# Block-sorted attention and a residual MLP: exponentials from rows of scores, turned by transposing DMAs

## The chip, the cores and the metric

One Trainium2 chip, one of its cores. The metric is the device time of one execution in microseconds. The engines of a core are PE (matrix products), DVE (vector), ACT (activations), POOL (here element-wise sums and the issue of loads) and SP (which here only issues DMAs). Each engine works through its own instructions in order; they wait for each other and for DMAs by semaphores.

## What is computed

Four batches, eight heads, 768 tokens, 64 columns per head; the tokens form 8 blocks of 96. `P` is an 8x8 matrix per head, made from `sort_net` by five rounds of normalising rows and columns.

```python
k_sorted = np.einsum('bhij,bhjcd->bhicd', P, k_b)      # blocks of k and v mixed by P
v_sorted = np.einsum('bhij,bhjcd->bhicd', P, v_b)
scores = scale * np.matmul(q_b, k_sb.transpose(0, 1, 2, 4, 3))   # 96x96 in each block
scores = scores - np.max(scores, axis=-1, keepdims=True)
attn = np.exp(scores)
attn = attn / (np.sum(attn, axis=-1, keepdims=True) + 1e-09)
x = np.matmul(attn, v_sb)                              # then heads side by side: 768x512
# residual MLP
a1 = alpha1 * x + beta1
tok = np.einsum('ts,bsd->btd', w_tok, a1)              # 768x768 over the tokens
u = x + lam * tok
a2 = alpha2 * u + beta2
ch = np.maximum(a2 @ w_ch1, 0.0) @ w_ch2               # 512 -> 2048 -> 512
out = u + lam * ch
```

## The kernel before

The batches run in a pipeline written out by hand. Batch 0's attention opens the program. Then, for b = 0, 1, 2, the function `both` does two thirds of the MLP of batch b (`hidden` for its first half of tokens, three `result` tiles, `hidden` for its second half) and, woven into it, the attention of batch b+1. After that `join` does the last three `result` tiles of batch b together with the token mix (`token_mix`) of batch b+1, and woven into that, `ahead` mixes the blocks of k and v of batch b+2. The MLP of batch 3 ends the program alone.

`weave(main, other, ratio)` sets the order: each step of a generator yields a cost, and after each step of `main` steps of `other` are recorded until their costs reach `ratio` times those of `main`. The costs only place instructions in the engines' queues; they delay nothing by themselves.

Attention of a batch, before. Heads are handled in pairs `p` = 0 to 3 (heads p and p+4 on the two halves of the partitions), and blocks in groups `g` of four. `score` computes q times k for eight 96x96 blocks into a PSUM bank pair `psA` (two exist, `bankA` takes them in turn), with the queries on the partitions; DVE reduces their maxima into `mx` (L453). When all eight scores of the batch are done, `split_max` and `turn_max` write the maxima as two bfloat16 parts and turn them (L474 to L482). Then `soft` computes the scores a second time with the keys on the partitions (L508), subtracts each query's maximum by a second product, with a mask of -1 (L515), and ACT takes eight 96x96 exponentials in one instruction into `ET` (L520). `value` multiplies `ET` by the sorted v, whose extra column of ones gives the sums (L534), and DVE divides into `x16` (L546, L547). The token mix reads `x16` (L609).

`hidden` makes one of 16 tiles of 128 hidden columns in each step: four products into one of the three PSUM banks of `psM` (L674), and a relu that empties the bank, on ACT (L684), for every fourth tile on DVE (L682). In stage 0, the first half's `hidden` also turns the second half of u (`u_turn`, with its activation L645 on ACT). `result` sums 16 products of 512 columns (L712), and two DVE instructions and an output store on SP follow (L721 to L723).

SP's queue holds, in one order, the output stores, the transposing DMAs for `a2T` (L656, after ACT's cast of u, L651), those for `qT` (`q_send`, L343), and `v_relay`, which sends the sorted v through DRAM to its place in `vS` (L430, L436). The loads of k, v and q of batch b+2 are issued by POOL behind a small copy, `gate` (L850), in the middle of `both`.

Of the kernel before, what the change touches and what calls it, by code (L numbers as in the profile page):

```python
# [10 lines left out]
FT = mybir.dt.float32  # L11
F16 = mybir.dt.float16
BF = mybir.dt.bfloat16
AF = mybir.ActivationFunctionType
ALU = mybir.AluOpType
# [5 lines left out]
def kernel(  # L21
# [18 lines left out]
    B, H, S, D = q.shape  # L40
    NB = sort_net.shape[-1]
    BLK = S // NB
# [20 lines left out]
    def wt(shape, dtype, name):  # L63
        return wts.tile(shape, dtype, name=name, tag=name)
# [4 lines left out]
    def tmp(shape, dtype, name, bufs):  # L69
        return work.tile(shape, dtype, name=name, tag=name, bufs=bufs)  # L70

    turn_A, turn_M = count(), count()

    def bankA():
        return psA.tile([128, 2, 512], FT, name="psA", tag=f"psA{next(turn_A) % 2}")

    def bank(pool, dtype=FT):
        n = 512 if dtype is FT else 1024
        tag = "psM" if pool is psM else "psX"
        return pool.tile([128, n], dtype, name=tag, tag=tag)  # L80
# [11 lines left out]
    kT = wt([128, H4 * S + 32], F16, "kT")  # L92
    qT = [[wt([128, S + 32], F16, f"qT{n}_{p}") for p in range(H4)] for n in range(2)]
    vS = two([BLK, 64, VP], F16, "vS")
    ET = [wt([BLK, 2, NB, GAP], F16, f"ET{n}") for n in range(2)]
    x16 = two([128, NT, C], F16, "x16")
    mh = wt([BLK, 2, 2, H4 * NB], BF, "mh")
    E0 = [ET[0][:], ET[1][:]]
    for home in (
        x16[1][0:BLK].rearrange("p s c -> p (s c)"),  # L100
        raw0[0:BLK, 0:2 * NB * GAP],
    ):
        E0.append(home.rearrange("p (l i c) -> p l i c", l=2, c=GAP))
    u = {}
    u16 = wt([128, NT, C], BF, "u16")
    w_tokT = wt([128, NT, S], BF, "w_tokT")
# [1 line left out]
    W2 = wt([128, HT, C], BF, "W2")  # L108
    PB = [wt([128, 2, 2, H4, NB], F16, f"PB{b}") for b in range(B)]

    def load_k(b):
        G.dma_start(rawk[0:64, :], k[b].rearrange("h (j t) d -> (h j) (t d)", j=NB)[:, 0:HALF * D])
        G.dma_start(rawk[64:128, :], k[b].rearrange("h (j t) d -> (h j) (t d)", j=NB)[:, HALF * D:])

    def load_v(b, halves=(0, 1)):
        src = v[b].rearrange("h (j t) d -> (h j) (t d)", j=NB)
        if b == 0:
            G.dma_start(raw0[0:64], src)
            return
        for th in halves:  # L120
            G.dma_start(
                rawv[th * 64:(th + 1) * 64, :], src[:, th * HALF * D:(th + 1) * HALF * D]
            )
# [46 lines left out]

    load_v(1, (0,))
    for home in E0[1:3]:
        G.memset(home[:, :, :, BLK:], 0.0)
    for quarter in range(4, 16):
        if quarter == 12:
            load_v(1, (1,))
# [7 lines left out]
        for p in range(H4):  # L184
            V.memset(qT[n][p][:, S:], 0.0)
    V.memset(v0T[:, BLK * D:], 0.0)
    V.memset(ET[0][:, :, :, BLK:], 0.0)
    ones_bf = wt([128, 1], BF, "ones_bf")
    V.memset(ones_bf[:], 1.0)

# [7 lines left out]
    mx0 = wt([BLK, 2, 2, H4 * NB], FT, "mx0")  # L198
    V.memset(mx0[:], 0.0)
    mx1 = wt([BLK, 2, H4 * NB], FT, "mx1")  # L200
    mx = [mx0[:, :, 0], mx1[:]]
    tp = [wt([128, BLK], BF, f"tp{n}") for n in range(2)]
    tp_of = {}
# [142 lines left out]
            )  # L346

    def q_two(b, p, eng):
        ps = psA.tile([128, 2, 1024], F16, name="psA", tag=f"psA{next(turn_A) % 2}")
        q_turn(b, p, ps[:, 0])  # L350
        q_turn(b, p + 1, ps[:, 1])
        q_copy(b, p, ps[:, 0], A)
        q_copy(b, p + 1, ps[:, 1], eng)
# [88 lines left out]
    def score(b, p, g):  # L442
        ps = bankA()
        for i in range(4):
            for hl in range(2):
                r = slice(hl * 64, hl * 64 + 64)
                c = (g * 4 + i) * BLK
                PE.matmul(  # L448
                    ps[:, hl, i * BLK:(i + 1) * BLK], qT[b % 2][p][r, c:c + 128],
                    kT[r, p * S + c:p * S + c + BLK], start=True, stop=True,  # L450
                )
        c = p * NB + g * 4
        V.tensor_reduce(  # L453
            mx[b % 2][:, :, c:c + 4],
            ps[0:BLK, :, 0:4 * BLK].rearrange("p l (i t) -> p l i t", t=BLK), AXX, ALU.max,
        )

    def score_one(b, p, g, hl):
        ps, r = bank(psM), slice(hl * 64, hl * 64 + 64)
# [9 lines left out]
            ps[0:BLK, 0:4 * BLK].rearrange("p (i t) -> p i t", t=BLK), AXX, ALU.max,  # L469
        )  # L470

    def split_max(b):
        m = mx[b % 2]
        V.tensor_copy(mh[:, :, 0], m)  # L474
        V.tensor_tensor(mh[:, :, 1], m, mh[:, :, 0], ALU.subtract)

    def turn_max(b):
        ps = bank(psX, BF)
        PE.transpose(
            ps[:, 0:BLK], mh[:].rearrange("p l e c -> p (l e c)"), identbf[0:BLK, 0:BLK]  # L480
        )
        V.tensor_copy(tp[b % 2][:], ps[:, 0:BLK])  # L482
        for p in range(H4):
            tp_of[p] = tp[b % 2]

    def turn_first(p, n):
        ps = bank(psX)
        PE.transpose(
# [8 lines left out]
            )  # L497

    def exps(b, p):
        return ET[p % 2] if b > 0 else E0[p]  # L500

    def soft(b, p, g):
        ps = bankA()
        for i in range(4):
            c = (g * 4 + i) * BLK
            for hl in range(2):
                r = slice(hl * 64, hl * 64 + 64)
                PE.matmul(  # L508
                    ps[:, hl, i * BLK:(i + 1) * BLK], kT[r, p * S + c:p * S + c + 128],
                    qT[b % 2][p][r, c:c + BLK], start=True, stop=False, skip_group_check=True,  # L510
                )
            for hl in range(2):
                r = slice(hl * 64, hl * 64 + 64)
                n = p * NB + g * 4 + i
                PE.matmul(  # L515
                    ps[:, hl, i * BLK:(i + 1) * BLK],
                    nmask[r, n:n + 1].to_broadcast([64, 128]), tp_of[p][r, :],
                    start=False, stop=True, skip_group_check=True,
                )
        A.activation(  # L520
            exps(b, p)[:, :, g * 4:(g + 1) * 4, 0:BLK],
            ps[0:BLK, :, 0:4 * BLK].rearrange("p l (i t) -> p l i t", t=BLK),
            AF.Exp, scale=scale,
        )

    def products(b, p, hl, ps):
        h = hl * H4 + p
        E = exps(b, p)[:, hl].rearrange("p i c -> p (i c)")
        for s in range(NT):
            b0, s3 = s // 3 * 4 + s % 3, s % 3  # L530
            for half in range(2):
                i = b0 + half
                c0 = i * GAP + (32 * s3 if half == 0 else 32 * s3 - BLK)
                PE.matmul(  # L534
                    ps[:, s * VP:s * VP + D + 1], E[:, c0:c0 + 128],
                    vS[b % 2][:, h * NB + i, 0:D + 1],
                    start=(half == 0), stop=(half == 1), skip_group_check=True,
                )
# [14 lines left out]
    def attention(b):  # L553
        yield 0.7
        if b + 1 < B:
            big_p(b + 1)
            yield 0.1
        for p in range(H4):
            for g in range(2):
                score(b, p, g)  # L560
            yield 0.65
        split_max(b)
        yield 0.9
        turn_max(b)
        yield 0.5
        for p in range(H4):
            for g in range(2):
                soft(b, p, g)
            yield 0.9
            if p > 0:  # L570
                value(b, p - 1)
                yield 1.1
        yield 0.5
        value(b, H4 - 1)

    def ahead(b):
# [93 lines left out]
    def hidden(b, half):  # L670
        for m in range(HT):
            ps = bank(psM)
            for ci in range(CT):
                PE.matmul(  # L674
                    ps[:, 0:TOK], W1[:, ci, m * 128:(m + 1) * 128], a2T_of[b, half][:, ci, :],
                    start=(ci == 0), stop=(ci == CT - 1),
                )
            if m % 2 == 0:
                pair = tmp([128, S], BF, "hT", 10)
            t = hT_of[m] = pair[:, m % 2 * TOK:(m % 2 + 1) * TOK]  # L680
            if m % 4 == 3:
                V.tensor_scalar(t, ps[:, 0:TOK], 0.0, None, op0=ALU.max)  # L682
            else:
                A.activation(t, ps[:, 0:TOK], AF.Relu)  # L684
            if b == 0 and half == 0 and m in (5, 7, 9, 11):
                u_turn(b, 1, (m - 5) // 2)
            yield 0.65
# [80 lines left out]
    q_pair(0, 3, psM, A)  # L768
    v_first(3, A, psM)
    v_first_layout(0, 3, A)  # L770
    G.memset(E0[3][:, :, :, BLK:], 0.0)
    load_q(1)
    load_k(1)
    for ci in range(CT):
# [59 lines left out]
    for b in range(B):  # L834
# [8 lines left out]
            break  # L843

        def both(b=b):
            yield from hidden(b, 0)
            for kk in range(3):
                yield from result(b, 0, kk, b if b > 0 and kk == 1 else None, 1)
                if kk == 1 and b + 2 < B:
                    G.tensor_copy(  # L850
                        gate[:], a2T_of[b, 1][0:1, CT - 1, 0:1] if b else vS[1][64:65, 63, 0:1]
                    )
                    load_v(b + 2)
                    load_k(b + 2)
                    load_q(b + 2)
            yield from hidden(b, 1)
            if b + 2 < B:
                q_send(b + 2)

        weave(both(), attention(n), 0.42)  # L860

        def join(b=b, n=n):
            yield from mixing(n, (0,))
# [6 lines left out]
            yield from result(b, 1, 2, n)  # L870
            yield from mixing(n, (5,))

        weave(join(), ahead(n + 1), 0.45)


# [28 lines left out]
```

## Time and profile before

| | |
|---|---|
| device time, three runs | 285.68, 285.9, 287.98 us (median 285.9) |
| the profiled execution's own time | 286.69 us |
| its span, first to last instruction | 284.9 us |
| granted PE clock, mean | 0.982 |
| 512 hidden products (L674) | 89.7 us of PE |
| 351 result products (L712) in the trace | 82.5 us of PE |
| 256 second scores and 256 subtractions (L508, L515) | 15.2 and 15.1 us of PE |
| 96 relus on ACT, 32 on DVE | 46.4 and 17.7 us |
| 28 + 4 exponentials of 96x768 (L520) | 24.2 us of ACT |
| DMA traffic | 31.01 MB, 58902 packets |

PE's busy time is the union of its instructions, which overlap: two products that work on different halves of the array run together. A group's row reads: line, engine, operation, output <- input, shapes, count, then the busy time, the mean duration in ns of one, and the idle time of its engine ahead of it with what ended that. A row of the chain of waits reads: start, length, engine, tile, line. A row of the timeline reads: start, length, engine, line, operation, output <- input, count, and in brackets the idle time ahead.

### The profile page before, as it was taken

What the parts mean: (1) busy time and instruction counts of PE and PEld (TensorE: products, weight loads), DVE (VectorE), ACT (ScalarE), POOL (GpSimd) and SP (SyncE); (2) the same over time, 40 slices, a digit from 0 to 9 for tenths busy, and PEclk for the clock granted to TensorE, in tenths of its full rate; (3) what the DMA queues carried; (4) which work ended last, traced back from release to release, by engine and by line L of the source; (5) the groups of instructions that cost most, each with busy time, mean ns of one, the idle gap of its engine ahead of it and who ended that gap; (6) DMA issues with size and microseconds to landing.
All of it is one profiled execution on the core that took longest, in us unless ns stands there. A gap on an engine that the chain in (4) does not pass through costs nothing.

```text
span 284.9 us, 6866 instructions
## 1 busy us (share of the span) xinstructions
PE 270.6 (95%) x2909; PEld 160.1 (56%) x2926; DVE 175.8 (62%) x340; ACT 126.4 (44%) x217; POOL 76.7 (27%) x96
## 2 busy tenths in 40 slices
PE   8968989799999999999999999999999999999995
PEld 6647864465566554455556554555566444645644
DVE  7887769987244469894553669792644587244124
ACT  3295847866425464243345474334344113512500
POOL 8399729103620270000074730000000900000000
PEclk9985899999999999999999999999999999999999
DMA  6998999997997102795169954880110033012002
GB/s 114 221 206 188 165 210 187 256 181 64 203 185 142 11 18 59 199 99 73 39 129 200 135 112 138 120 133 4 70 43 2 18 96 91 0 21 102 9 37 76
DMA packets 58902, 31.01 MB, mean 109 GB/s; under 512 B 48412, under 2 KB 53688, under 8 KB 58808
## 3 DMA queue, kind: packets, MB, share of 16 engines
q0 software_dynamic: 19408, 14.81, 34.9%
q1 hardware_dynamic: 39464, 15.76, 27.8%
q8 instruction: 23, 0.38, 0.6%
q14 instruction: 7, 0.06, 0.1%
HBM read 32.79 MB, written 8.65 MB: 145 GB/s over the span
## 4 chain that ended last, share of the span: by engine, by line
PE 79%; DVE 9%; DMA 4%; POOL 3%; issue 2%; ACT 2%; DVEq 0%; POOLq 0%
PE psM L712 28%; PE psM L674 28%; PE psM L609 9%; DMA u<-in_v_dram 4%; PE psA L534 3%; DVE mx L453 3%; PE psA L508 2%; PE psA L515 2%; PE psA L448 2%; DVE x L547 1%; PE psM L695 1%; POOL u L162 1%; DVE u L622 1%; PE psA L393 1%; PE psA L423 1%
## 5 line engine op out<-in xcount | busy, mean ns | idle before, releaser
L674 PE MATMUL psM<-a2T,W 128*128 128x384 bf16 x512 | 89.7, 326 | 0.4 <-ACT a2T L645 0.2
L712 PE MATMUL psM<-W,hT 128*128 128x512 bf16 x351 | 82.5, 379 | 1.5 <-issue 1.0
L684 ACT ACTIVATE hT<-psM 128x384 bf16<-128x384 f32 x96 | 46.4, 490 | 62.5 <-PE psM L674 61.0
L674 PEld LDWEIGHTS <-W 128*128 128x128 bf16 x512 | 48.1, 98 | 33.2 <-issue 2.2
L712 PEld LDWEIGHTS <-hT 128*128 128x128 bf16 x368 | 34.7, 98 | 39.6
L617 POOL TENSOR_TENSOR u<-x,rb 128x512 f32<-128x512 f16 x24 | 29.5, 1257 | 76.6 <-DVE x L547 73.0
L721 DVE TENSOR_TENSOR tmix<-psM,lamB 128x512 f32<-128x512 f32 x23 | 15.9, 690 | 35.6 <-PE psM L712 35.6
L682 DVE TENSOR_SCALAR hT<-psM 128x384 bf16<-128x384 f32 x32 | 17.7, 554 | 28.8 <-PE psM L674 24.8
L609 PE MATMUL psM<-x,w_tokT 128*128 128x512 f16 x144 | 34.4, 379 | 0.6 <-DVE x L547 0.6
L520 ACT ACTIVATE ET<-psA 96x768 f16<-96x768 f32 x28 | 21.1, 802 | 28.0 <-PE psA L515 28.0
L453 DVE TENSOR_REDUCE mx<-psA 96x8 f32<-96x768 f32 x30 | 27.2, 947 | 3.2 <-PE psA L448 3.1
L651 ACT CAST u<-u 128x512 bf16<-128x512 f32 x24 | 14.8, 619 | 28.3 <-DVE u L622 28.3
L609 PEld LDWEIGHTS <-w_tokT 128*128 128x128 bf16 x144 | 13.7, 98 | 16.3 <-DVE x L547 1.1
L622 DVE TENSOR_TENSOR u<-u,tmix 128x512 f32<-128x512 f32 x24 | 20.2, 842 | 3.2 <-DVE tmix L621 0.5
L722 DVE TENSOR_TENSOR u<-u,tmix 128x512 f32<-128x512 f32 x23 | 16.9, 734 | 1.6
L621 DVE TENSOR_TENSOR tmix<-psM,a1lB 128x512 f32<-128x512 f32 x24 | 16.4, 684 | 2.1 <-PE psM L609 2.0
L547 DVE TENSOR_TENSOR x<-psA,recip 128x768 f16<-128x768 f32 x16 | 15.3, 957 | 0.6
L508 PE MATMUL psA<-qT,kT 64*128 64x96 f16 x256 | 15.2, 212 | 0.2 <-ACT ET L520 0.2
L508 PEld LDWEIGHTS <-kT 64*128 64x128 f16 x256 | 12.4, 98 | 5.2 <-issue 5.1
L129 POOL DMA_DIRECT2D qn<-in_q_dram x16 | 13.3, 851 | 7.5 <-DMA rawk<-in_k_dram 6.7
L515 PE MATMUL psA<-tp,nmask 64*128 64x96 bf16 x256 | 15.1, 211 | 0.0
L546 DVE RECIPROCAL recip<-psA 128x12 f32<-128x12 f32 x16 | 3.7, 230 | 17.8 <-PE psA L534 17.8
(123 smaller groups left out, 270.4 us busy)
## 6 DMA issues: line engine op xcount, KB each, us to landing
out_dram<-u SPq DMA_DIRECT2D x23, 256.0 KB
W<-in_moe_w_ch_dram POOLq DMA_DIRECT2D x8, 512.0 KB, 19.7
rawk<-in_k_dram POOLq DMA_DIRECT2D x8, 384.0 KB, 8.3
rawv<-in_v_dram POOLq DMA_DIRECT2D x6, 384.0 KB, 5.9
vscr<-rawv SPq DMA_DIRECT2D x3, 768.0 KB
qn<-in_q_dram POOLq DMA_DIRECT2D x4, 384.0 KB, 6.5
qn<-in_q_dram POOLq DMA_DIRECT2D x16, 96.0 KB, 9.4
vS<-vscr SPq DMA_DIRECT2D x8, 192.0 KB
```

The costliest lines, as they stand in the source:

```text
L453: V.tensor_reduce(mx[b % 2][:, :, c:c + 4], ps[0:BLK, :, 0:4 * BLK].rearrange("p l (i t) -> p l i t", t=BLK), AXX, ALU.max,)
L508: PE.matmul(ps[:, hl, i * BLK:(i + 1) * BLK], kT[r, p * S + c:p * S + c + 128], qT[b % 2][p][r, c:c + BLK], start=True, stop=False, skip_g ...
L515: PE.matmul(ps[:, hl, i * BLK:(i + 1) * BLK], nmask[r, n:n + 1].to_broadcast([64, 128]), tp_of[p][r, :], start=False, stop=True, skip_grou ...
L520: A.activation(exps(b, p)[:, :, g * 4:(g + 1) * 4, 0:BLK], ps[0:BLK, :, 0:4 * BLK].rearrange("p l (i t) -> p l i t", t=BLK), AF.Exp, scale ...
L547: V.tensor_tensor(x16[b % 2][:].rearrange("p s (l h d) -> p l s h d", l=2, d=D)[:, :, :, p], xg[:, :, :, 0:D], recip[:].unsqueeze(3).to_br ...
L609: PE.matmul(ps[:], w_tokT[:, ks, kt * 128:(kt + 1) * 128], x[:, ks, :], start=(ks == 0), stop=(ks == NT - 1),)
L617: G.tensor_tensor(ub[:, kt], x[:, kt], rb[:, kt], ALU.add)
L622: V.tensor_tensor(ub[:, kt], ub[:, kt], t[:], ALU.add)
L674: PE.matmul(ps[:, 0:TOK], W1[:, ci, m * 128:(m + 1) * 128], a2T_of[b, half][:, ci, :], start=(ci == 0), stop=(ci == CT - 1),)
L682: V.tensor_scalar(t, ps[:, 0:TOK], 0.0, None, op0=ALU.max)
L684: A.activation(t, ps[:, 0:TOK], AF.Relu)
L712: PE.matmul(ps[:], hT_of[m][:, kk * 128:(kk + 1) * 128], W2[:, m, :], start=(m == 0), stop=(m == HT - 1),)
```

## The change

For batches 1 to 3 the second scores go, with the split and the turn of the maxima. Instead, DVE multiplies the maxima of each score by -scale into `nmx`, and ACT takes the exponential straight from the first scores, one 96x96 block per instruction, with the block's column of `nmx` as bias. The result has the queries on the partitions (`rows`, three slots of 96x1024 in the `x16` of the other parity); for each score one transposing DMA on SP turns its eight blocks into `ET` (`exp_send`). `ET` gets a layout by groups for that. Batch 0 keeps its path.

The steps of `attention` have new costs: each score, then its exponentials in two halves, then its transpose; the value of pair p - 2 is computed inside pair p. Also changed: the relus alternate between ACT and DVE, in the last MLP too; the costs of `both`'s steps (0.5, 0.8, 0.7 in place of 0.65, 0.86, 0.65) and its ratio (0.45 for 0.42), and `join`'s ratio (0.35 for 0.45); and from batch 2 on the loads of k and v are issued as four DMAs each, in runs of 256 elements, every second run by the same DMA.

```diff
+    def short(ap):
+        return ap.rearrange("r (a e x) -> r a e x", e=2, x=4 * D)
+
     def load_k(b):
+        if b > 1:
+            src = k[b].rearrange("h (j t) d -> (h j) (t d)", j=NB)
+            for th in range(2):
+                for e in range(2):
+                    G.dma_start(
+                        short(rawk[th * 64:(th + 1) * 64, :])[:, :, e],
+                        short(src[:, th * HALF * D:(th + 1) * HALF * D])[:, :, e],
+                    )
+            return
...
+    nmx = wt([BLK, 2, H4 * NB], FT, "nmx")
...
     def score(b, p, g):
...
+        if b > 0:
+            V.tensor_scalar(
+                nmx[:, :, c:c + 4], mx[b % 2][:, :, c:c + 4], -scale, None, op0=ALU.mult
+            )
+        return ps
+
+    def exp_rows(b, p, g, hl, ps):
+        E = rows(b, p, g)
+        for i in range(4):
+            c = p * NB + g * 4 + i
+            A.activation(
+                E[:, hl * 4 + i, 0:BLK], ps[0:BLK, hl, i * BLK:(i + 1) * BLK],
+                AF.Exp, bias=nmx[:, hl, c:c + 1], scale=scale,
+            )
+
+    def rows(b, p, g):
+        home = x16[1 - b % 2][0:BLK].rearrange("p s c -> p (s c)")
+        n = (p * 2 + g) % 3
+        return home[:, n * 1024:(n + 1) * 1024].rearrange("p (n c) -> p n c", c=128)
+
+    def exp_send(b, p, g):
+        SP.dma_start_transpose(
+            ET[p % 2][:, g * 8:(g + 1) * 8, 0:BLK],
+            rows(b, p, g).rearrange("p n c -> p (n c)"),
+        )
...
         for p in range(H4):
             for g in range(2):
-                score(b, p, g)
-            yield 0.65
-        split_max(b)
-        yield 0.9
-        turn_max(b)
-        yield 0.5
-        for p in range(H4):
-            for g in range(2):
-                soft(b, p, g)
-            yield 0.9
-            if p > 0:
-                value(b, p - 1)
-                yield 1.1
-        yield 0.5
+                ps = score(b, p, g)
+                yield 0.3
+                for hl in range(2):
+                    exp_rows(b, p, g, hl, ps)
+                    yield 0.3
+                if g == 0 and p > 1:
+                    value(b, p - 2)
+                    yield 0.7
+                exp_send(b, p, g)
+        value(b, H4 - 2)
+        yield 3.0
         value(b, H4 - 1)
...
-            if m % 4 == 3:
+            if m % 2:
                 V.tensor_scalar(t, ps[:, 0:TOK], 0.0, None, op0=ALU.max)
...
         def both(b=b):
-            yield from hidden(b, 0)
+            for _ in hidden(b, 0):
+                yield 0.5
             for kk in range(3):
-                yield from result(b, 0, kk, b if b > 0 and kk == 1 else None, 1)
+                for _ in result(b, 0, kk, b if b > 0 and kk == 1 else None, 1):
+                    yield 0.8
...
-            yield from hidden(b, 1)
+            for _ in hidden(b, 1):
+                yield 0.7
...
-        weave(both(), attention(n), 0.42)
+        weave(both(), attention(n), 0.45)
...
-        weave(join(), ahead(n + 1), 0.45)
+        weave(join(), ahead(n + 1), 0.35)
```

`load_v` is changed as `load_k` is. In `products`, the column of `ET` follows the new layout.

## The prediction

> **What bounds the kernel now.** I read the busy shares first, then the table of stretches, then the chain of waits, then single rows. PE is busy 270.6 of 284.9 us at a granted clock of 1.00 in every stage that the change touches, and every other engine has room on average:
>
> ```profile
> PE 270.6 (95%) x2909; PEld 160.1 (56%) x2926; DVE 175.8 (62%) x340; ACT 126.4 (44%) x217; POOL 76.7 (27%) x96
> ```
>
> The work divides into three "attention stages" (the MLP of batch b woven with the attention of batch b+1, `both`), three joins, and a last MLP without attention. The first three rows below are the attention stages, cut at their first hidden matmul and at the first token mix after them (points from the chain of waits); the fourth is the same MLP work with no attention in it. The columns are the stretch, its length, busy time by engine, clock, DMA share.
>
> ```profile
> 57.19:98.17 40.98, 40.50 (x473) 24.66 (x476) 21.31 (x36) 20.26 (x37) 9.45 (x14) 1.00 1.05 136
> 118.93:159.83 40.90, 40.35 (x465) 24.05 (x466) 23.34 (x43) 17.96 (x33) 9.53 (x14) 1.00 0.92 112
> 180.59:221.57 40.98, 40.22 (x464) 24.02 (x465) 22.88 (x40) 17.96 (x33) 0.61 (x1) 1.00 0.33 56
> 240.21:271.31 31.10, 31.00 (x174) 17.12 (x175) 10.61 (x20) 12.27 (x25) 0.00 (x0) 1.00 0.11 38
> ```
>
> So attention adds 40.9 - 31.1 = 9.8 us to a stage, nearly all on PE. The chain of waits (start, length, what) prices its pieces:
>
> ```profile
> 128.41 0.45 PE psA L448 x16
> ...
> 140.24 0.74 PE psA L534 x24
> ...
> 157.13 0.75 PE psA L534 x24
> 157.87 1.95 PE psM L674 x12
> 159.83 1.29 PE psM L609 x6
> ```
>
> Two scores cost 0.45 us, one `value` 0.75. Two second scores (`soft`) run from 134.07 to 134.85 in the timeline, 0.78. A stage then has 4 x 0.45 + 4 x 0.78 + 4 x 0.75 = 7.9 us, 0.15 for the turn of the maxima, and 1.7 of handovers (scores come in pairs and wait for DVE's 0.95 us reductions to free psA). The last three rows matter later: after the last `value`, three hidden tiles (1.95 us) pass before the token mix, which needs that value's division on DVE.
>
> **Second scores, split and turn of the maxima (removed in three stages).** Gone from PE: 3.1 + 0.15 us a stage. Eight single scores take the place of four pairs; a lone score's extent is 0.34 against 0.225 in a pair, so 8 x 0.3 = 2.4 instead of 1.8, while half of the 1.7 of handovers goes, as scores now come some 4 us apart. PE's own stage: 31.1 + 2.4 + 3.0 + 0.8 = 37.3 us. That is the floor, 3.6 under 40.9.
>
> **64 exponentials of 96x96 instead of 8 of 96x768 (ACT).** No row has this form. The nearest are two groups and two pieces of the timeline:
>
> ```profile
> L684 ACT ACTIVATE hT<-psM 128x384 bf16<-128x384 f32 x96 | 46.4, 490 | 62.5 <-PE psM L674 61.0
> L520 ACT ACTIVATE ET<-psA 96x768 f16<-96x768 f32 x28 | 21.1, 802 | 28.0 <-PE psA L515 28.0
> ...
> 55.91 0.67 ACT L645 ACTIVATE a2T<-psM,cols 128x384 bf16<-128x384 bf16 x1
> 56.48 0.66 ACT L645 ACTIVATE a2T<-psX,cols 128x384 bf16<-128x384 bf16 x1
> ```
>
> The first two give (802 - 490)/384 = 0.81 ns per column and 178 ns fixed: 256 ns for 96 columns. `L645`, with two per-partition operands, takes 0.67 at 384 columns, 90 ns more for each; the bias makes it 345 ns alone. Back to back they overlap: two L645 start at 55.91 and 56.48, and two relus end in 0.86 instead of 0.98. The closest of these is L645, 0.57 to 0.47 apart (two of them in 1.14 us), less 288 columns x 0.81: 240 ns. I take 240, bounds 190 (overlap as in the relus) and 345 (none). A stage gets 64 x 0.24 = 15.4 us, and half the relus stay on ACT (16 x 0.49 = 7.8): 23 of 37 us. On average it fits. DVE gets 8 more relus (8 x 0.55) and 8 small multiplies (0.2 each), 29 of 37 us.
>
> The Trainium skill (ScalarE: Activation LUTs, What ACT_TABLE_LOAD costs) gives 280 ns + 0.833 ns per column for an activation with a pointer as bias and 93 ns of overlap: 360 alone, 267 in a row. By that the sum below would end an estimated 1.5 us later.
>
> It fits worst in the first `hidden`, where scores 0 to 3 fall, one in four tiles. Per four tiles PE needs 4 x 0.65 + 0.3 = 2.9 us and ACT 2 x 0.49 + 8 x 0.24 = 2.9: even. Behind an exponential on ACT stands the next relu, for which psM's three buffers wait; PE can run two tiles (1.3 us) ahead. A score's reduction and multiply end 1.2 us after it, the queue is then about 0.5 late, and slack is about 0.4. I take 0.3 us of stall in stages 1 and 2 (bounds 0 and, at 345 ns, 3 x 0.84 = 2.5). In stage 0 four L645 (0.5 to 0.67 each) stand between the exponentials, 2.3 us more for ACT against some 0.9 of u_turn on PE: 1.4 us (0.5 to 4).
>
> **Eight transposing DMAs a stage, on SP.** They replace nothing. A lone transpose of 128x512 shows its delay:
>
> ```profile
> 250.75 1.19 SPq L656 DMA_TRANSPOSE a2T<-u  x1
> ...
> 253.35 0.96 DVE L664 TENSOR_SCALAR a2T<-a2T,cols 128x384 bf16<-128x384 bf16 x3 [2.40 <-DMA a2T<-u]
> ```
>
> 1.2 us on the queue and 2.6 from issue to use; 96x1024 is 1.5 times the data, call it 2.9. In stages 1 and 2 they stand behind v_relay's stores, the last three a2T transposes and an output store:
>
> ```profile
> 118.22 5.27 SPq L436 DMA_DIRECT2D vS<-vscr  x4
> 123.60 4.28 SPq L656 DMA_TRANSPOSE a2T<-u  x2
> 127.97 0.54 SPq L723 DMA_DIRECT2D out_dram<-u  x1
> 128.57 1.98 SPq L656 DMA_TRANSPOSE a2T<-u  x1
> ```
>
> SP comes free at 130.55, 11.6 us into the stage. The first transpose lands at 14.5; the exponentials of score 3 reuse its rows (three slots) and wait for it, 8 x 0.24 more, 16.5. `value(0)` needs that psA bank and comes up on PE at 11.6 (16 tiles, 4 scores) + 3.4 + 0.3 + 0.9 = 16.2. I take 0.4 us of stall, 0 to 3 if the transposes take twice as long. Later ones have room: score 5's rows land near 25.1 and value(2) uses them near 27.8; score 7's near 32, value(3) near 35.5. In stage 0 no a2T transpose is ahead, but the relay's data (the gate on POOL waits for them until 68.1) and the loads are: 0.4 too.
>
> **Short runs, the weave's costs and ratios.** k and v loads issue four DMAs each instead of two, at the same bytes; the gate for them opens where it did. POOL pays 4 x 0.55 us, and the q loads after them wait for more landings, hidden by a join of 20 us before q's scores. The changed program's order of instructions has one step that is not free: the last value now stands before the last hidden tile in stages 0 and 1 (two tiles in stage 2). Reciprocal 0.23 + multiply 0.96 + some 0.15 of handover against one tile of 0.65: 0.7 us idle ahead of the token mix, covered by 1.95 before. Thinner `ahead` in the joins: 0, PE bounds them (20.7 us measured, 20.5 summed). The relus moved to DVE in the last MLP: 0, since a pair of tiles takes PE 1.3 us and each engine under 0.6.
>
> **Sum.** Stage 0: 37.3 + 1.4 + 0.4 + 0.7 = 39.8, 1.2 saved. Stage 1: 37.3 + 0.3 + 0.4 + 0.7 = 38.7, 2.2 saved. Stage 2: 37.3 + 0.3 + 0.4 = 38.0, 3.0 saved. 286.7 (the profiled execution, span 284.9) - 6.4 = 280.3. The median of the runs shown is 285.9, 0.8 lower, so 279.5 from there; I say 280.
>
> **Rivals.** (1) *All of it hides*: exponentials near 190 ns, the transposes on time. Stages at 37.3: 286.7 - 11 = 275.7. For: ACT averages 62%. Against: the even count in the first hidden. (2) *ACT eats half the gain*: near 290 ns a period is 3.3 us against PE's 2.9, 1.2 lost per stage in the first hidden, 0.5 later where score 5 and 7 wait for banks: 280.3 + 5 = 285.5, within 1% of before. (3) *ACT becomes the bound*: at 345 ns no overlap, 2.5 us in each first hidden and some 1.5 after it: 280.3 + 12 - 1 of slack = 291. It decides from about 320 ns on. For: relus that stand alone show their full 0.49. Against: the overlaps read above. (4) *Transposes held up by the loads, slower*: stage 0 has a DMA share of 1.05 and stage 1 of 0.92, and no row shows a transpose while k, v, q come in. If each lands 4 us later, value(0) loses 3.5 and value(2) 1.3 in stages 0 and 1, with 2 in stage 2 from the relay's tail: 280.3 + 11.6 = 292. It costs more than it brings from about 2 us of delay a step. The Trainium skill (DMA: Bandwidth & Descriptors, Issuing engines are not separate DMA queues) speaks for it: all queues share the same 16 engines and interleave. No run here shows how much.
>
> **How the numbers follow.** Forecast (277 to 283.5) 0.48, (1) 0.14, (2) 0.17, (3) 0.10, (4) 0.11. Over 1%, about what a measurement tells from no change, is under 283 or above 288.8: faster 0.62, same 0.17, slower 0.21. The range from 275 to 289.5 holds the forecast, (2) and most of (1); the forecast's own is 277 to 283.5.
>
> **What would show it.** Right: stages near 39.8, 38.7 and 38.0 us; exponentials of 0.34 in the row's mean but about 0.24 apart; a gap of 0.7 us before the token mix at two stage ends; first hidden of stage 0 longest. Wrong: relus waiting on ACT with PE idle in all three (ACT), value rows waiting for ET from a DMA (transposes), or stages still at 41.

## The result, and the profile after

The changed kernel takes 289.2 us in the median (287.0 to 290.6), the kernel before 286.9 (285.7 to 288.3) on the same chips: a ratio of 1.0071 with a 95% interval of 1.0047 to 1.0095. It is 0.7% slower. 280 was forecast. Executions over 1.5% longer than the fastest of the same kernel are left out of all times and ratios here.

The profiled execution of the changed kernel takes 290.59 us with a span of 288.2. First its page: the busy row of the engines, the chain of waits summed by engine, and two groups (out<-in, shapes, count | busy, mean ns of one | idle before them and what ended most of it).

```profile
PE 268.1 (93%) x2539; PEld 153.2 (53%) x2539; DVE 195.1 (68%) x387; ACT 137.6 (48%) x353; POOL 83.5 (29%) x104
...
PE 66%; DMA 15%; DVE 9%; ACT 5%; POOL 3%; issue 2%; ACTq 0%; DVEq 0%; POOLq 0%
...
L487 ACT ACTIVATE x<-psA,nmx 96x96 f16<-96x96 f32 x192 | 47.6, 351 | 21.7 <-DVE nmx L478 15.4
...
L566 PE MATMUL psA<-vS,ET 96*128 96x65 f16 x336 | 13.4, 193 | 6.4 <-DMA ET<-x 5.0
```

PE has 370 records fewer (387 by its weight loads: the trace of the kernel before lacks 17 of the result products), as the change takes away, and ACT, the engine that the forecast feared for, stands at 48%. What is new is in the second and the last row: a DMA holds 15% of the chain, and `value`'s matmuls wait for `ET`, written by the transposes. The table of stretches for the three attention stages, cut at the same points as before (stretch, length, busy time by engine, granted clock, DMA share, GB/s), says in which stage:

```profile
58.44:102.79 44.35, 38.99 (x347) 21.93 (x347) 26.97 (x50) 25.08 (x85) 12.06 (x17) 1.00 1.36 157
123.71:164.82 41.11, 38.17 (x339) 21.24 (x337) 28.53 (x57) 23.04 (x81) 12.05 (x17) 0.99 1.11 139
186.92:224.69 37.77, 37.53 (x337) 21.00 (x335) 27.93 (x53) 23.16 (x81) 0.00 (x0) 1.00 0.66 99
```

Before they were 40.98, 40.90 and 40.98. Stage 2 gained 3.2 us, stage 1 nothing (it lost 0.2), stage 0 lost 3.4. ACT and DVE do much the same work in all three. What differs is POOL's column: in stages 0 and 1 it issues 17 times (the gate, and the loads of the batch after next), in stage 2 never. The rest of the 3.3 us of span is 1.34 in join 1 (22.10 against 20.76, of which below), 1.25 in the opening, ahead of the new path, and 0.3 in the other joins and the end. In the opening the granted clock stands at 0.50 for 3.4 us from 51.2 on in this execution and not in that of the kernel before; the last section says what makes it fall.

The chain of waits (start, length, what) of stage 1 names the wait:

```profile
146.73 6.07 DMA ET<-x
...
152.84 0.73 PE psA L566 x18
153.57 0.86 PE psM L703 x6
154.44 8.29 DMA ET<-x
...
162.77 0.75 PE psA L566 x18
```

Two transposes hold the chain for 6.1 and 8.3 us, and behind each stands a `value`; between them the chain has 0.86 us of hidden tiles. The prediction had 2.9 us for one. PE has other hidden tiles to do while these transposes are under way. In stage 1 it stands idle for long only behind the second, ahead of the last value:

```profile
162.77 0.73 PE L566 MATMUL psA<-vS,ET 96*128 96x65 f16 x18 [2.38 <-DMA ET<-x]
```

In stage 2 no transpose is in the chain at all. The waits of the whole execution (what waits <- for what: sum, number, longest), and ACT's longest wait for a transpose, in stage 0, in the timeline:

```profile
ACT x L487 <- DMA ET<-x: 6.2, 2, 5.4
...
PE psA L566 <- DMA ET<-x: 5.0, 3, 2.4
...
PE psM L638 <- DVE x L579: 1.7, 3, 0.7
```

```profile
83.81 1.94 ACT L487 ACTIVATE x<-psA,nmx 96x96 f16<-96x96 f32 x8 [5.44 <-DMA ET<-x]
```

The exponentials of a later score reuse rows that a transpose has not read yet; ACT stands for 5.44 us, and what is queued behind them too.

### The profile page after: what moved, and what is told of

Read it like the earlier page. It is cut to its first block, busy times and chain, and to the rows that moved or that the text cites. A ratio compares the mean times of both kernels' runs of the same rounds, so it can differ in the third digit from the quotient of the medians.

```text
span 288.2 us, 6398 instructions
## 1 busy us (share of the span) xinstructions
PE 268.1 (93%) x2539; PEld 153.2 (53%) x2539; DVE 195.1 (68%) x387; ACT 137.6 (48%) x353; POOL 83.5 (29%) x104
## 4 chain that ended last, share of the span: by engine, by line
PE 66%; DMA 15%; DVE 9%; ACT 5%; POOL 3%; issue 2%; ACTq 0%; DVEq 0%; POOLq 0%
PE psM L741 22%; PE psM L703 22%; DMA ET<-x 11%; PE psM L638 10%; DMA u<-in_v_dram 4%; ACT x L487 3%; DVE mx L473 2%; DVE x L579 2%; PE psA L566 2%; PE psA L468 2%; PE psM L724 1%; POOL u L181 1%; PE psM L430 1%; PE psA L413 1%; PE psA L443 1%
## 5 line engine op out<-in xcount | busy, mean ns | idle before, releaser
L741 PE MATMUL psM<-W,hT 128*128 128x512 bf16 x368 | 84.8, 379 | 0.0
L487 ACT ACTIVATE x<-psA,nmx 96x96 f16<-96x96 f32 x192 | 47.6, 351 | 21.7 <-DVE nmx L478 15.4
L713 ACT ACTIVATE hT<-psM 128x384 bf16<-128x384 f32 x64 | 31.8, 500 | 53.7 <-PE psM L703 49.5
L741 PEld LDWEIGHTS <-hT 128*128 128x128 bf16 x368 | 34.6, 98 | 39.7
L711 DVE TENSOR_SCALAR hT<-psM 128x384 bf16<-128x384 f32 x64 | 35.5, 555 | 28.6 <-PE psM L703 24.7
L638 PE MATMUL psM<-x,w_tokT 128*128 128x512 f16 x144 | 36.2, 397 | 1.7 <-DVE x L579 1.7
L473 DVE TENSOR_REDUCE mx<-psA 96x8 f32<-96x768 f32 x30 | 28.3, 948 | 7.1 <-PE psA L468 6.7
L566 PE MATMUL psA<-vS,ET 96*128 96x65 f16 x336 | 13.4, 193 | 6.4 <-DMA ET<-x 5.0
L566 PEld LDWEIGHTS <-ET 96*128 96x128 f16 x336 | 12.4, 97 | 9.3 <-DMA ET<-x 5.6
L148 POOL DMA_DIRECT2D qn<-in_q_dram x16 | 13.2, 827 | 10.3 <-DMA rawk<-in_k_dram 6.2
L179 ACT CAST kT<-psA 64x512 f16<-64x512 f32 (+1 forms) x18 | 11.3, 628 | 5.6 <-PE psA L413 4.8
L179 ACT CAST rawv<-psA 128x1024 f16<-128x1024 f32 x7 | 7.1, 1009 | 12.7 <-PE psA L443 12.7
```

The lines of the kernel that those rows point to most:

```text
L179: A.copy(dst, src)
L473: V.tensor_reduce(mx[b % 2][:, :, c:c + 4], ps[0:BLK, :, 0:4 * BLK].rearrange("p l (i t) -> p l i t", t=BLK), AXX, ALU.max,)
L487: A.activation(E[:, hl * 4 + i, 0:BLK], ps[0:BLK, hl, i * BLK:(i + 1) * BLK], AF.Exp, bias=nmx[:, hl, c:c + 1], scale=scale,)
L566: PE.matmul(ps[:, s * VP:s * VP + D + 1], E[:, c0:c0 + 128], vS[b % 2][:, h * NB + i, 0:D + 1], start=(half == 0), stop=(half == 1), skip_ ...
L638: PE.matmul(ps[:], w_tokT[:, ks, kt * 128:(kt + 1) * 128], x[:, ks, :], start=(ks == 0), stop=(ks == NT - 1),)
L741: PE.matmul(ps[:], hT_of[m][:, kk * 128:(kk + 1) * 128], W2[:, m, :], start=(m == 0), stop=(m == HT - 1),)
```

## The experiments

The theory (A) after these readings: a transpose that runs while k, v and q are loaded lands several us late. Its rivals: (B) ACT's or DVE's own work is the bound, and a late transpose only what is seen last; (C) SP issues the transposes late, behind other DMAs. The stage lengths of all runs, from the chains of waits, are in a table at the end of this section.

**No loads beside the transposes.** The changed kernel without the loads of batches 2 and 3, whose attention then works on old data:

```diff
-                    load_v(b + 2)
-                    load_k(b + 2)
-                    load_q(b + 2)
```

> The changed kernel with the loads of k, v and q of batches 2 and 3 left out (these batches then work on old data). Theory A (transposes wait for the loads): stages 0 and 1 shorten from 44.4 and 41.1 us to about 39 and 38, as stage 2 has 37.8; the token mix after stage 1 no longer finds a lowered clock; total about 280 to 281, 2 to 3% under the kernel before. Rival B (ACT and DVE are too full in stages 0 and 1): stages stay within 1 us of 44.4 and 41.1, total 288 to 289.

Measured: 281.26 us, 0.982 of before (0.976 to 0.987). The stretches of stages 0 and 1:

```profile
58.65:98.70 40.05, 38.37 (x344) 21.76 (x346) 26.70 (x50) 24.98 (x85) 0.18 (x1) 1.00 0.71 114
119.63:158.18 38.55, 37.57 (x336) 21.11 (x337) 28.54 (x57) 22.86 (x81) 0.17 (x1) 1.00 0.79 117
```

ACT's and DVE's busy times are what they were, and the stages are 4.3 and 2.6 us shorter. SP issues the last two transposes of stage 1 no earlier than before. First with the loads, then without:

```profile
150.20 5.51 SPq L498 DMA_TRANSPOSE ET<-x  x2
```

```profile
146.12 5.44 SPq L498 DMA_TRANSPOSE ET<-x  x2
```

Both rows begin 26.5 us into the stage. That speaks for (A) and against (B) and (C). Join 1 fell from 22.10 to 20.92.

**k and v in long runs, as before the change.** The change minus its `short` branches:

```diff
-        if b > 1:
-            src = k[b].rearrange("h (j t) d -> (h j) (t d)", j=NB)
...
-                    G.dma_start(
-                        short(rawk[th * 64:(th + 1) * 64, :])[:, :, e],
```

> The changed kernel with the k and v loads in long runs, two DMAs each, as before. If long descriptors are what holds up a transpose, stages 0 and 1 grow by 2 us or more each (total 292 to 295). If the engines' total load counts and not the length of a run, no difference beyond 1 us (288 to 290). Rival B expects no difference either.

Measured: 295.21 us, 1.030 of before (1.025 to 1.035). Stage 1, and the transpose that its chain waits for:

```profile
123.35:170.29 46.94, 39.61 (x336) 22.15 (x336) 28.62 (x57) 22.97 (x81) 8.93 (x13) 0.93 1.17 128
```

```profile
146.36 12.54 DMA ET<-x
```

The same bytes in runs of 3072 elements in place of 256 hold one transpose for 12.5 us. So the short runs, which the prediction costed at nothing, are worth some 6 us to the changed kernel (295.21 - 289.17 = 6.0, or 6.6 by the two ratios to the kernel before). Nearly all of it is in stage 1; stage 0 took 45.27 us, 0.9 more.

**The new path for batch 3 alone,** whose stage has no loads; batches 1 and 2 take the old path, with the old loads, costs and ratios.

```diff
-        if b > 0:
+        if b == B - 1:
             V.tensor_scalar(
                 nmx[:, :, c:c + 4], mx[b % 2][:, :, c:c + 4], -scale, None, op0=ALU.mult
...
+        if b < B - 1:
+            for p in range(H4):
+                for g in range(2):
+                    score(b, p, g)
```

> The new path for batch 3 alone, whose stage 2 has no loads beside it; batches 1 and 2, their costs, ratios, relus and loads as before. Theory A: stages 0 and 1 at 41, stage 2 at 37.8, total 3 us under the kernel before, ratio 0.989 (0.985 to 0.993). If the change gains nothing by itself: ratio 1.00.

Measured: 283.87 us, 0.990 (0.986 to 0.993). Stages 40.97, 40.90 and 37.96: the 3.0 us of one stage, with nothing paid for them.

**Loads put into the stage that had none.** Batch 3's loads are issued once more in stage 2; nothing reads them.

```diff
-                if kk == 1 and b + 2 < B:
+                if kk == 1:
...
-                    load_v(b + 2)
-                    load_k(b + 2)
-                    load_q(b + 2)
+                    load_v(min(b + 2, B - 1))
+                    load_k(min(b + 2, B - 1))
+                    load_q(min(b + 2, B - 1))
```

> The changed kernel with the loads of k, v and q of batch 3 issued a second time in stage 2, at the same point as in stage 1; nothing reads them. Theory A: stage 2 grows from 37.8 to about 41, with waits of the last two values for ET from a DMA; total 3 us over the changed kernel (291 to 293). Rival B: stage 2 stays at 37.8, total as the changed kernel.

Measured: 294.48 us, 1.027 (1.024 to 1.031). Stage 2, and its chain:

```profile
184.49:228.30 43.81, 39.03 (x336) 21.51 (x336) 27.94 (x53) 23.12 (x81) 13.26 (x19) 0.97 1.14 137
```

```profile
215.08 9.88 DMA ET<-x
```

37.8 became 43.8: the direction of (A), and twice the price that it had named. With the first experiment this is the cause shown from both sides.

**Which of the loads: without q's, and without k's and v's.** One execution each, read by their stages.

```diff
 e5_no_q                        e6_no_kv
                     load_v(b + 2)                  -                    load_v(b + 2)
                     load_k(b + 2)                  -                    load_k(b + 2)
-                    load_q(b + 2)                                       load_q(b + 2)
```

> The changed kernel without the loads of q of batches 2 and 3 (old data is used); k and v stay. Theory A says nothing yet on which load holds the transposes. If it is the many short packets of q: stages 0 and 1 (first hidden product to token mix, in the chain of waits) fall from 44.4 and 41.1 to near the 40.1 and 38.6 without any loads. If it is the bytes of k and v: they fall by no more than a third of the way.

> The changed kernel without the loads of k and v of batches 2 and 3 (old data is used); q stays. The counterpart of the run without q: if q's packets hold the transposes, stages 0 and 1 stay within 1 us of 44.4 and 41.1; if k and v do, they fall to near 40.1 and 38.6.

Measured: 286.44 us without q's, 280.69 without k's and v's. Stage 1 of the one, then of the other:

```profile
119.66:161.60 41.94, 38.93 (x337) 21.50 (x336) 28.50 (x56) 22.87 (x81) 5.46 (x9) 0.98 1.07 144
```

```profile
117.67:156.45 38.78, 37.67 (x338) 21.11 (x336) 28.63 (x57) 22.78 (x81) 6.79 (x9) 1.00 1.10 136
```

The DMA shares are nearly equal, 1.07 and 1.10, and the stages 3.2 us apart. q's loads alone, in runs of 64 elements, cost the transposes nothing (38.78 against 38.55 with no load at all); k's and v's alone give stage 1 the whole loss. Stage 0 took 41.41 without q's and 40.05 without k's and v's. Whether q's loads cost anything there beside k's and v's can't be told from one execution each: with all the loads the stage took 44.35 in one kernel and 42.47 in another.

**Loads moved out of the way.** Batch 1 keeps the old path, so that stage 0 can take loads as before; q of batch 3 is loaded there too. k and v of batch 3, in long runs again, wait until the last transpose of stage 1 has landed.

```diff
+                if kk == 1 and b == 0:
+                    G.tensor_copy(gate[:], vS[1][64:65, 63, 0:1])
                     load_v(b + 2)
                     load_k(b + 2)
                     load_q(b + 2)
+                    load_q(b + 3)
...
+            if b == 1:
+                G.tensor_copy(gate[:], ET[1][0:1, 15, BLK - 1:BLK])
+                load_v(b + 2)
+                load_k(b + 2)
```

> A version of both kernels: batch 1 on the old path with its stage, batches 2 and 3 on the new path; q of batch 3 is loaded in stage 0 right after q of batch 2, and k and v of batch 3 only when the last transpose of stage 1 has landed, with the mixing of v in the join after it begun later; the last value of stage 1 comes two tiles earlier. Theory A: stage 0 41, stage 1 38, stage 2 37.8, ratio to the kernel before 0.98 (0.975 to 0.985). If the transposes were slow for another reason than loads beside them, stage 1 stays at 41 and the ratio at 0.99; if the later loads hold up the join, stage 1 gains and join 1 loses the same.

Measured: 281.55 us, 0.983 (0.978 to 0.987); stages 40.96, 37.87 and 38.9. It beats both kernels. Stage 2 lost 1 us to v's relay, which now ends later on SP, ahead of the first transpose: its chain has a `191.81 2.97 DMA ET<-x`.

**Shorter runs in the changed kernel: 128 elements, then 64, then 64 with the last value brought forward.**

```diff
 e8_runs_128
-        return ap.rearrange("r (a e x) -> r a e x", e=2, x=4 * D)
+        return ap.rearrange("r (a e x) -> r a e x", e=2, x=2 * D)
 e9_runs_64
+        return ap.rearrange("r (a e x) -> r a e x", e=4, x=D)
...
-                for e in range(2):
+                for e in range(4):
 e10_runs_64_v: e9, and
-        yield 3.0
+        yield 2.6
         value(b, H4 - 1)
```

> The changed kernel with the k and v loads in runs of 128 elements instead of 256, two DMAs a half. Theory A2 (a transpose's packets take turns with the loads' packets on a DMA engine, so the length of a load's packet sets its delay; q's runs of 64 elements delay nothing that is seen): stages 0 and 1 fall from 44.4 and 41.1 to about 42 and 39.5, total near 285. Rival D (what counts is that k and v write 64 partitions at a time, or their bytes): stages as in the changed kernel.

> The changed kernel with the k and v loads in runs of 64 elements as q's, four DMAs a half. Theory A2: stages 0 and 1 near the 40.1 and 38.6 without k and v loads, total 281 to 282, unless the loads now land too late for the joins (then joins 0 and 1 grow from 20.9 by what the mixing of v waits). Rival D: stages 44 and 41 or longer, since the same bytes in more packets last longer.

> The run before with the last value of a stage two tiles earlier (cost 2.6 instead of 3.0). The gap ahead of the token mix (0.7 us after stages 0 and 1) goes: 1.4 us less than the run before, if the last transpose has landed by then; else the same.

Measured: 289.78, 292.04 and 290.94 us; ratios 1.010 (1.002 to 1.019), 1.018 (1.009 to 1.027) and 1.010 (1.003 to 1.018). 128 elements brought nothing: stages 44.6 and 41.5, a miss, and join 1 grew to some 24.5 us with a `148.83 12.70 DMA rawk<-in_k_dram` in its chain. 64 shortened stage 1 to some 39.2 us (39.7 in `e10_runs_64_v`), but then the loads themselves land too late. The chain of waits of `e9_runs_64` in join 1:

```profile
160.80 3.97 DMA qn<-in_q_dram
```

POOL is through with k's DMAs 35.6 us into stage 1, at 156.6; in the changed kernel it was 29.1. Join 1 takes 27.1 us in place of 22.1. The value brought forward was to save up to 1.4 us, which the overlapping intervals of the last two do not show; stage 0 took 45.0 there, with `88.50 8.35 DMA ET<-x` in the chain, against 41.8 in `e9_runs_64`. Thinner loads moved the wait from the transposes to the loads.

**The relay earlier, in the kernel with the loads moved; and that kernel with k and v of batch 3 in runs of 256.**

```diff
 e11_relay_early, against e7_loads_moved
-        if b == 1:
+        if b != 2:
             v_relay(b)
...
-            if n + 1 < B:
+            if n == 1:
                 v_relay(n + 1)
 e12_relay_runs, against e11_relay_early: the short branches again, under
+        if b > 2:
```

> The version with the loads moved, in which stage 2 took 38.9 us (its first transpose waited on SP behind the relay of v). Here the relay of batch 3 stands right after the mixing of v, ahead of an output store that waits for DVE. If SP's order is what held stage 2: stage 2 falls to 37.8 and the ratio from 0.9825 to about 0.979. If the loads in long runs beside the a2T and qT transposes are: no change.

> The same with the moved loads of k and v of batch 3 in runs of 256 elements, as in the changed kernel. If long runs beside transposes are what costs in the join: 0.5 to 1 us less than with long runs. If the loads then only land later for the mixing in the join: 0.5 to 2 us more.

Measured: 281.08 us, 0.980 (0.976 to 0.984), with a profiled span of 279.0; and 283.97, 0.990 (0.986 to 0.994). The first is the fastest version that does all the loads, though not told from `e7_loads_moved` by the time. Stage 2 went from 38.9 to about 38.3 us and not to 37.8, so SP's order was, by one execution each, about half of what held it. With none of the attention's transposes left beside them, the long runs are the better ones: with runs of 256 join 1 grew to some 23.4 us (21.1 with long runs), and its chain has a `155.46 8.25 DMA rawv<-in_v_dram`.

The stages, in us (about, where the chain does not show the first tile itself):

| | stage 0 | stage 1 | stage 2 |
|---|---|---|---|
| before | 40.98 | 40.90 | 40.98 |
| forecast | 39.8 | 38.7 | 38.0 |
| after | 44.35 | 41.11 | 37.77 |
| e1, no loads | 40.05 | 38.55 | 37.77 |
| e2, long runs | 45.27 | 46.94 | 37.76 |
| e3, batch 3 alone | 40.97 | 40.90 | 37.96 |
| e4, loads in stage 2 too | 42.47 | 41.13 | 43.81 |
| e5, no q | 41.41 | 41.94 | 37.76 |
| e6, no k, v | 40.05 | 38.78 | 37.76 |
| e7, loads moved | 40.96 | 37.87 | about 38.9 |
| e8, runs of 128 | 44.58 | about 41.5 | about 37.8 |
| e9, runs of 64 | 41.76 | about 39.2 | about 37.8 |
| e10, runs of 64, value | 44.98 | about 39.7 | about 37.8 |
| e11, relay early | about 41.0 | 37.90 | about 38.3 |
| e12, runs of 256 | about 41.0 | about 38.6 | about 38.3 |

The same loads beside the same code leave stage 0 at 44.35 in one execution (after) and at 42.47 in another (e4), so differences of 2 us in that stage alone say little.

## Why the prediction was wrong, step by step

**Second scores, split and turn of the maxima: right.** 3.6 us off the floor, 3.0 off stage 2 was forecast; stage 2 gave 3.2, and 3.0 in the kernel that changes only that stage.

**The exponentials on ACT: right.** One was put at 345 ns alone and 240 in a row. The group shows 351, and eight in a row end in 1.94 us: (1.94 - 0.35) / 7 = 227 ns apart. Without loads the stages are 40.05, 38.55 and 37.77, where 39.8, 38.7 and 38.0 stood in the sum. The stalls put down to ACT, 1.4 us in stage 0 and 0.3 after it, had about the right size too: without loads PE waits there for ACT's and DVE's activations and relus for 1.1 us in stage 0 and 0.2 in each of the others. Rivals (1), (2) and (3) all turned on this price and fall with it. By the figures of the Trainium skill (ScalarE: Activation LUTs, What ACT_TABLE_LOAD costs) one takes an estimated 360 ns alone, which agrees with 351, and an estimated 267 in a row, which 227 does not bear out.

**The last value ahead of the token mix: right.** 0.7 us was the price; PE waits 0.66 us ahead of the token mix at the end of stage 0 and 0.47 at the end of stage 1 (the third of the three waits above is batch 0's).

**The first transpose on SP: right enough, late was another.** It was due 11.6 us into stage 1 and was issued at 133.03, 9.3 us into it. SP's order costs nothing that the chain shows.

**Transposes that come later "have room": the step that failed.** The sum took 2.9 us for every transpose, from a lone one of `a2T` in a part of the kernel without loads, and 0.4 us of stall in stage 0. Under k's and v's loads the chain has 6.1 and 8.3 us for one, and the room (2.7 us ahead of value(2), 3.5 ahead of value(3)) is gone: PE waits 2.36 us for value(2) in stage 0 and 2.38 for value(3) in stage 1. Against the same kernel without loads this costs 44.35 - 40.05 = 4.3 us in stage 0, 41.11 - 38.55 = 2.6 in stage 1 and 22.10 - 20.92 = 1.2 in join 1, together 8.0; the medians say 289.17 - 281.26 = 7.9.

This is rival (4), with the right mechanism in stages 0 and 1 and a price of 11.6 that was not the measured one: it counted 2 us for a relay in stage 2 which did not hold anything up, and 3.5 a stage for value(0), which waits in neither. It had 0.11 and stood at 292; that 289.2 lies inside the stated range of 275 to 289.5 is luck, since the one case that had the loads hold up the transposes lay outside it. The prediction knew that no row showed a transpose beside loads, and still made the forecast from the one row without them; the DMA shares of 1.05 and 0.92 in the two stages were the rows nearest to the case, and spoke for the other end of the bounds. The Trainium skill (DMA: Bandwidth & Descriptors, Issuing engines are not separate DMA queues) named the mechanism, one set of engines for all queues. The runs agree that the loads delay the transposes, but not that sharing sets the price: at nearly equal DMA shares in stage 1 (1.07 and 1.10) k's and v's loads cost 3.4 us there and q's 0.2.

**Short runs, put at nothing: mis-sized.** They are worth some 6 us to the changed kernel, which takes 295.2 without them.

**Open.** From 3072 to 256 elements in a run, and from 128 to 64, stage 1 gets shorter, and from 256 to 128 it does not. The last section has what the packets say of that; it fits the first step and the last, and leaves the second open.

## What to carry to other kernels

A DMA whose landing a matmul waits for is priced with the loads that run in the same window, and where the trace has no such row, the forecast should not rest on a row without loads; here the late end of the bounds was the nearer one. Move the loads out of its window rather than thin them: moved, the same idea, in two of the three stages, is 2.0% faster than the kernel before; thinned further, it stayed slower, and with runs of 64 the loads' own landing became the wait. Before a new path is put everywhere, put it where nothing else competes: one stage without loads brought its full 3 us at once.

## What the hardware showed that was not expected

After the second late transpose of stage 1 the granted clock of TensorE fell to half. Stretches of 1 us of the changed kernel, PE alone (stretch, length, PE busy, granted clock, DMA share, GB/s), first in stage 0, then at the end of stage 1:

```profile
91.00:92.00 1.00, 0.05 (x2) 1.00 1.60 159
92.00:93.00 1.00, 0.00 (x0) 1.00 1.60 206
```

```profile
161.00:162.00 1.00, 0.00 (x0) 1.00 1.41 174
162.00:163.00 1.00, 0.23 (x8) 1.00 2.38 153
163.00:164.00 1.00, 1.00 (x21) 0.91 2.41 153
164.00:165.00 1.00, 0.53 (x3) 0.50 2.42 154
165.00:166.00 1.00, 1.00 (x3) 0.50 2.39 152
...
167.00:168.00 1.00, 1.00 (x6) 0.88 2.07 143
```

PE idles for 2.4 us both times (91.0 to 93.4, 160.4 to 162.8). The first cost only itself; after the second the clock stands at 0.50 from 164 to 167, and join 1 takes 1.2 us more (in `e2_long_runs`, where the clock fell inside stage 1, join 1 took 20.92). Without loads there is no such idle time, and the join's clock is 1.00. The Trainium skill (TensorE: Matmul & The Clock Gate, Part 1) has a free-running window of some 3.4 us, over which the activity counts: an equal gap can then count once and not the next time, by where it lies. The traces agree. In each of the fourteen the clock changes only at points that lie a whole number of 3.41 us apart; here it falls at 51.2 and at 163.8, each time for 3.41 us. Between 42 and 260 us of all the traces, PE was idle for 1.82 us or more of each of the 15 such stretches at whose end the clock fell, and for 1.81 at most of the 850 others at full clock. The gap of stage 1 lies whole in one stretch (160.4 to 163.8, PE idle 2.36 us); that of stage 0 is cut in two, 1.10 and 1.26. In the opening it is 1.82 us of 47.8 to 51.2, where the kernel before has 1.18 at most. A short stall can so cost half as much again as its own length, in the stage after.

The second thing is that the length of a load's runs, at the same bytes, sets how long a transpose beside it takes: in stage 1 the chain's longest is 12.5 us in runs of 3072 elements and 8.3 in runs of 256 (up to 10.3 in stage 0 of the kernel without q's loads). The packets in the traces, counted by queue, say how. The last transpose but one of stage 1 writes 768 packets of 256 bytes. Without loads they start in 1.15 us (147.29 to 148.44 of `e1_no_loads`), beside the loads in 3.9 (154.66 to 158.54 of the changed kernel). While both have work, POOL's queue and SP's move packet for packet: from 159 to 161 us 493 of the loads and 481 of the transposes. So the transposes go at the pace of the loads' packets, and longer ones make it slower. In one microsecond the transposes move

| a load's run, elements | its packet, bytes | transposes' packets in 1 us | where |
|---|---|---|---|
| 3072 | 6144 | 32 | e2, 150 to 151 |
| 256 | 512 | 248 | after, 160 to 161 |
| 128 | 256 | 339 | e8, 159 to 160 |
| 64 | 128 | 414 | e9, 92 to 93 |

This fits what e2 lost, and q's loads, in runs of 64, which cost next to nothing. It does not give the whole wait. In e8 the same 768 packets took 3.9 us too (152.98 to 156.87), where 339 a microsecond would make 2.3; and the transpose's first packet came 3.3 us after its issue beside the loads (150.20 to 153.49 of the changed kernel) and 0.4 without them. No run shows why.
